# Diagonal blocks stored turned, the first two units substituted in buffers of their own, and a new hand-written order, in a delta-rule attention followed by a token and channel mixer

## The chip, the cores and the metric

The kernel runs on one core of a Trainium2 chip, in float32. The core has a matrix engine (PE; its weight loads are listed as PEld), a vector engine (DVE), a scalar engine (ACT), a general engine (POOL) and a queue that issues transfers (SP). Each engine runs its own instructions in the order in which the program lists them and waits for the others by semaphores. The metric is the device time of one execution in microseconds (us).

## The reference

First an attention block: per batch and head a state of 48x48 is updated token by token, each key normalized. Then a mixer: a low-rank product over tokens and a two-layer network over channels.

```python
B, H, S, D = 4, 8, 768, 48
k_n = k / (np.linalg.norm(k, axis=-1, keepdims=True) + 1e-06)
for t in range(S):
    y[:, :, t] = q[:, :, t] @ state                       # per batch and head
    v_old = state.T @ k_n[:, :, t]
    state = state + beta[t] * outer(k_n[t], v[t] - v_old)
x = y.transpose(0, 2, 1, 3).reshape(B, S, H * D)          # (4, 768, 384)
u = x + ((x.transpose(0, 2, 1) @ U) @ V).transpose(0, 2, 1)   # U (768, 32), V (32, 768)
out = u + np.maximum(u @ w_ch1, 0.0) @ w_ch2              # 384 -> 1536 -> 384
```

## The kernel before

**Chunks and units.** Tokens are cut into 12 chunks of 64 per batch. A *unit* is six chunks of one batch with all eight heads; there are eight units, n = 0 to 7, two per batch, and units take turns in two large buffers, `slots` (slot 0 for even n, slot 1 for odd n). Within a chunk the token-by-token update is written as a triangular system of 64x64 (keys times keys, scaled by beta), whose inverse is needed; then the chunk's effect on the state is a few matmuls.

**Preparing a unit.** Loads of k, q, v (`load`, `name` "z" is a second copy of odd heads of k) go to the slot. For units 0 to 2, PE turns k and q (`turn`, L672) and ACT and DVE copy the result (`placed`, L682 to L687); later units are turned by DVE (`turn_blocks`, L747). `products` (L700) multiplies keys with keys (i = 0) and keys with queries (i = 1), for two halves j of the heads. For i = 0 the two 32x32 diagonal blocks of each 64x64 product are brought into a tile `diag` (L710 on ACT for the upper block, L713 twice on DVE for the lower one, with a mask `even`); ACT then copies the whole product (L720) and, for units 0 and 1, splits it by rows (L724). For i = 1 DVE masks the product (L731), once per parity of the heads.

`blocks` inverts the diagonal blocks. A DVE transposition (L794) spreads them so that each partition holds one block in `gs`; `norms` takes the norms from their diagonals (ACT's square root L619, five small DVE steps L622 to L627, the turned norms L633, the scaling of v L636); L798 scales; then `substituted` runs size - 1 steps, each a DVE product (L803) and a DVE subtraction (L809), on `gs` and `xt`. For units 0, 1 (`SPLIT`) and 2 (`QUARTERED`) the blocks are halved first, 15 steps on 16x16; the others do 31 steps on 32x32. POOL clears `xt` beforehand (`seed`, L788). L816 transposes the inverse back into `zz`, and L825 makes its turned copy. All units use the same `gs`, `xt`, and one buffer for the products of the steps.

`joins` puts the inverses together to 64x64: for the halved units with two rounds of small matmuls (L860, L874) with ACT copies (L835, L865) and a DVE step (L878) between; for all with four phases of 32x32 matmuls (L900/L903, L918/L921), ACT copies between them (L908, L927, L939) and POOL clears (L946). `prepare` applies the inverse to k and v (L1023, L1034 on PE; L1042, L1047 on ACT).

**The recurrence** (`recur`) walks through the 12 chunks of a batch: L1072 (PE) and L1085 (DVE) make z from the state s, L1100 (PE) and L1111 (DVE; L1113 for the first) the next state, L983 and L997 the outputs, which ACT puts into X (L967). The chunks 0 to 5 need unit 2b, the chunks 6 to 11 unit 2b + 1.

**Weights.** U, V and the two layers' weights come in as pairs of words (L1186; 14 pieces, i = 0 for U, 1 for V, then 6 and 6) and are converted by one ACT scaling (L1198) and three DVE passes (L1212, L1219, L1226). A landing buffer serves several pieces in turn, so a later load waits for an earlier piece's last pass. The second layer is then combined by eight DVE differences (L1141).

**The mixer** of a batch starts when its 12 chunks are in X: `front` (L1393, L1399, L1412, L1417, L1436, L1439), then the channels (L1497, relu L1462) and the second layer (L1617, L1537) for three blocks of 256 tokens. While batch b is mixed, batch b + 1 goes through preparation and recurrence on the same PE. For the last batch, L1296 and L1617 run alone at the end.

**The order.** Every routine yields its next step, and a table `ORDER` says which routine's step is emitted at each place; 2259 places. `run` only follows the table (the costs in `op(...)` don't decide anything any more). Since each engine works in emission order, the table is what sets each engine's queue.

## Time and profile before

| | us |
|---|---|
| time, median of three runs | 599.11 |
| the three runs | 602.46, 598.93, 599.11 |
| span of the profiled execution | 594.9 |
| PE busy, share | 559.7, 94% |
| DVE busy, share | 409.3, 69% |
| ACT busy, share | 216.8, 36% |
| POOL busy, share | 133.3, 22% |
| first matmul of the mixer's channels (L1497) starts at | 115.95 |
| granted PE clock 0.50 | 31.8 to 86.4 and 93.3 to 103.5 |

The span is one profiled execution, from its first to its last instruction; the runs' times are of executions of the whole program, and their median is 4.2 us above this span. Times in the text count from the span's start. Busy time of PE is a union over overlapping matmuls whose ends are modelled. The granted clock is the share of full speed that PE had. In rows of the groups, the figures behind the bar are busy us, mean ns of one instruction, and the idle time of the engine just before.

### The profile page before, as it was taken

Reading aid. Unit: us, or ns where it says so; the run is one execution under the profiler, and the core shown is the slowest. Engines: PE = TensorE matmul, PEld = TensorE weight load, DVE = VectorE, ACT = ScalarE, POOL = GpSimd, SP = SyncE. Lnnn points to the kernel's source line nnn. Section 1 sums busy time; section 2 is a strip of 40 time slices with the busy share of each in tenths; the row PEclk is TensorE's granted clock in tenths of the full one; section 3 lists DMA queues with packets and bytes.
Section 4 is the critical chain, followed back from the end, with each engine's and each line's share of the span. In section 5 each row is a group of like instructions: output and inputs, shape, how many; then the busy total and the mean of one; then the engine's idle time right before and its main releaser. Section 6 shows DMA issues by size and latency. Waiting matters only on the chain.

```text
span 594.9 us, 23426 instructions
## 1 busy us (share of the span) xinstructions
PE 559.7 (94%) x10428; PEld 481.6 (81%) x10428; DVE 409.3 (69%) x1011; ACT 216.8 (36%) x442; POOL 133.3 (22%) x229
## 2 busy tenths in 40 slices
PE   3778978899999999999999999999999999999997
PEld 3578977678988887989889887889899868656997
DVE  3888758899999458999884279998883235313542
ACT  1846475446322542035224341252243321335000
POOL 8122036116010724141205214520310000000000
PEclk9855556999999999999999999999999999999999
DMA  9981639714030415240402144420401000000000
GB/s 140 180 176 24 214 80 197 152 56 79 3 65 12 68 31 92 46 91 13 82 2 43 18 83 90 79 56 2 95 7 43 4 2 4 16 8 1 26 28 28
DMA packets 89445, 36.23 MB, mean 61 GB/s; under 512 B 75456, under 2 KB 87104, under 8 KB 89344
## 3 DMA queue, kind: packets, MB, share of 16 engines
q1 hardware_dynamic: 80800, 24.69, 20.7%
q0 software_dynamic: 6944, 9.74, 8.3%
q8 instruction: 82, 1.34, 1.0%
q10 hardware_dynamic: 1600, 0.30, 0.3%
q14 instruction: 19, 0.16, 0.1%
HBM read 29.98 MB, written 4.72 MB: 58 GB/s over the span
## 4 chain that ended last, share of the span: by engine, by line
PE 83%; DVE 11%; issue 2%; ACT 2%; DMA 1%; SPq 0%; DVEq 0%; ACTq 0%
PE P L1617 27%; PE P L1497 22%; PE P L1296 7%; PE P L700 4%; DVE xt L809 3%; DVE prod L803 3%; PE P L1072 2%; PE P L860 2%; PE P L874 2%; PE P L1023 2%; PE P L1034 2%; PE P L983 2%; PE P L997 2%; PE P L1100 2%; PE P L1412 2%
## 5 line engine op out<-in xcount | busy, mean ns | idle before, releaser
L1497 PE MATMUL P<-ut,w_sb 128*128 128x256 f32 x648 | 150.1, 385 | 1.5 <-ACT ut L1439 0.9
L1497 PEld LDWEIGHTS P<-ut,w_sb 128*128 128x128 f32 x648 | 119.9, 190 | 18.7 <-ACT ut L1439 1.1
L1617 PE MATMUL P<-w_sb,hs 128*128 128x192 f32 x540 | 96.7, 331 | 0.1
L1617 PEld LDWEIGHTS P<-w_sb,hs 128*128 128x128 f32 x540 | 87.2, 190 | 3.7 <-issue 1.2
L809 DVE TENSOR_TENSOR xt<-xt,prod 128x112 f32<-128x112 f32 (+21 forms) x200 | 64.6, 323 | 6.9
L803 DVE TENSOR_TENSOR prod<-gs,xt 128x112 f32<-128x112 f32 (+21 forms) x200 | 63.3, 316 | 3.5
L1537 DVE TENSOR_TENSOR X<-X,P 128x192 f32<-128x192 f32 x84 | 29.1, 349 | 49.8 <-PE P L1617 49.4
L1462 ACT ACTIVATE hs<-P 128x512 f32<-128x512 f32 x54 | 32.2, 598 | 77.5 <-PE P L1497 65.6
L967 ACT COPY X<-P 64x192 f32<-64x192 f32 x96 | 30.0, 313 | 66.3 <-PE P L997 63.4
L1617 PE MATMUL P<-w_sb,S 128*128 128x192 f32 x288 | 50.7, 330 | 0.0
L1617 PEld LDWEIGHTS P<-w_sb,S 128*128 128x128 f32 x288 | 46.6, 190 | 2.8 <-issue 1.8
L555 POOL DMA_DIRECT2D slot<-in_v_dram x32 | 21.1, 664 | 92.3 <-DVE prod L803 60.3
L1085 DVE TENSOR_TENSOR z<-slot,P 128x192 f32<-128x192 f32 x44 | 15.5, 352 | 30.8 <-PE P L1072 29.7
L541 POOL DMA_DIRECT2D slot<-in_q_dram x40 | 24.6, 621 | 46.9 <-DVE slot L747 33.3
L939 ACT COPY slot<-zz 32x384 f32<-32x384 f32 x64 | 32.4, 509 | 7.0 <-DVE zz L878 3.9
L700 PE MATMUL P<-slot 48*64 48x64 f32 x1536 | 30.9, 231 | 2.1 <-issue 1.4
L1296 PE MATMUL P<-slot,w_sb 128*128 128x384 f32 x96 | 32.9, 486 | 0.0
L700 PEld LDWEIGHTS P<-slot 48*64 48x64 f32 x1536 | 27.9, 144 | 5.6 <-issue 2.7
L946 POOL MEMSET slot<- 32x384 f32 x32 | 13.3, 421 | 84.2 <-PE P L903 63.4
L1617 PE MATMUL P<-w_sb,slot 128*128 128x192 f32 x180 | 30.4, 327 | 0.9 <-DVE X L1537 0.9
L555 POOL DMA_DIRECT2D slot<-in_k_dram x44 | 29.4, 670 | 8.3 <-PE P L1100 7.6
L1617 PEld LDWEIGHTS P<-w_sb,slot 128*128 128x128 f32 x180 | 29.3, 190 | 1.7 <-DVE X L1537 1.5
(153 smaller groups left out, 901.4 us busy)
## 6 DMA issues: line engine op xcount, KB each, us to landing
out_dram<-X SPq DMA_DIRECT2D x22, 192.0 KB, 2.7
w_sb<-in_moe_w_ch_dram SPq DMA_DIRECT2D x10, 384.0 KB, 5.6
slot<-in_k_dram SPq DMA_DIRECT2D x48, 72.0 KB, 3.9
slot<-in_k_dram POOLq DMA_DIRECT2D x44, 72.0 KB, 3.8
slot<-in_v_dram SPq DMA_DIRECT2D x32, 72.0 KB, 3.7
slot<-in_v_dram POOLq DMA_DIRECT2D x32, 72.0 KB, 3.5
X<-in_moe_w_ch_dram SPq DMA_DIRECT2D x6, 384.0 KB, 6.1
wide<-in_moe_w_ch_dram SPq DMA_DIRECT2D x6, 384.0 KB, 5.0
```

Source lines behind the costliest of these rows:

```text
L541: queue.dma_start(out=blocked(n)[quarter(y % 4), j, g, :, 0:w], in_=src[b, 4 * g + 2 * j + par, hf * UC * L : (hf + 1) * UC * L, BK * low ...
L555: queue.dma_start(out=t[half(1 - g if name == "z" else g), :, to, 0:D], in_=src[b, 4 * g + s, hf * UC * L : (hf + 1) * UC * L, :].rearrang ...
L700: nc.tensor.matmul(p_g[half(g ^ (par * i)), par, c], kq[rows, c, j, 0, half(g)], kq[rows, c, j, i, half(g)], start=True, stop=True,)
L803: nc.vector.tensor_tensor(out=prod, in0=gb[:, :, j : j + 1, j + 1 :].to_broadcast([128, split, m, w]), in1=xb[:, :, 0:m, j : j + 1].to_bro ...
L809: nc.vector.tensor_tensor(out=xb[:, :, 0:m, j + 1 :], in0=xb[:, :, 0:m, j + 1 :], in1=prod, op=ALU.subtract,)
L939: nc.scalar.copy(pg[quarter(i), :, at, :, a : a + BK], cut(zc, h)[quarter(i)].rearrange("p r (c j) t -> p r c j t", j=2),)
L967: nc.scalar.copy(x[half(c % 2), c // 2, 4 * D * g : 4 * D * (g + 1)].rearrange("p (j r d) -> p r j d", r=2, d=D), states(p_y)[half(g)],)
L1296: nc.tensor.matmul(to, w, t, start=start, stop=stop, skip_group_check=True)
L1462: nc.scalar.activation(hs[:, fs[0] : fs[1] + 1 : fs[1] - fs[0]], p_f, ACTF.Relu)
L1497: nc.tensor.matmul(p_f[:, x], w(x, t), ut[:, t], start=(t == 0), stop=(t == KT - 1))
L1537: nc.vector.tensor_tensor(out=to, in0=to, in1=p, op=ALU.add)
L1617: nc.tensor.matmul(to, of[0], of[1], start=of[2], stop=of[3], skip_group_check=True)
```

## The change

1. The tile `diag` holds its blocks with the element index outermost instead of innermost, so that the DVE transposition out of it reads consecutive elements. It is filled by four copies of 32 partitions each (for units 0 and 2 to 7 two on ACT and two on DVE, for unit 1 all on ACT) instead of one masked ACT pass and two masked DVE passes.
2. The transposition back reads `xt` in its own order and writes the turned copy in `zz` first; the other copy is made from it by the smaller transposition. For the halved units the ACT copies `part` start from the returned inverse directly.
3. The mask of q products is one DVE pass over both parities.
4. Unit 1 has its own two buffers (in a part of the second layer's weight tile that is not in use yet) and its own product buffer; the units' waits follow from that (`ahead`). Unit 2 waits for unit 0 there, later units for the one before.
5. For units 0 and 1 the product and the subtraction of a step are separate places of the table, so that other DVE instructions can stand between them.
6. `ORDER` is new as a whole, 2289 places. Unit 0's k is loaded first (SP's and ACT's first four issues), then unit 1's; POOL clears both units' buffers at the start, ahead of its loads; the load of U and its ACT scaling and first two DVE passes stand ahead of the diagonal copies. Unit 0's q products stand behind its joining on PE. All weights are converted and combined on DVE before the last chunk of batch 0's recurrence (before: after it too). The two preparations of unit 1 stand in one piece.

```diff
-        diag = slot[:, 6144 : 6144 + BK * BK].rearrange("p (q t) -> p q t", t=BK)
+        diag = slot[:, 6144 : 6144 + BK * BK].rearrange("p (t q) -> p q t", t=BK)
...
+    room = w2_sb.rearrange("p m f d -> p (m f d)")[:, 0 : 2 * (BK + 1) * BK].rearrange(
+        "p (z s t) -> p z s t", z=2, t=BK
+    )
+
+    def grams_of(n):
+        return room[:, 0] if n == 1 else gs
+
+    def inverse_of(n):
+        return room[:, 1] if n == 1 else xt
+
+    def ahead(n):
+        return n - 1 if n > 2 else -1 if n < 2 else 0
...
-                yield op("act", act(384) + 0.1, rush=True)
-                nc.scalar.mul(to, p_g[:, :, :, 0:BK], even[:, 0:1])
-                for r in range(2):
-                    yield op("dve", dve(192) + 0.05, rush=True)
-                    nc.vector.scalar_tensor_tensor(
-                        out=to[:, r], in0=p_g[:, r, :, BK:L], scalar=even[:, 1:2], in1=to[:, r],
-                        op0=ALU.mult, op1=ALU.add,
-                    )
+                for y in range(4):
+                    rows, cols = quarter(y), quarter(y % 2)
+                    if n == 1 or y % 2 == 0:
+                        yield op("act", act(384) + 0.05, rush=True)
+                        nc.scalar.copy(to[rows], p_g[rows, :, :, cols])
+                    else:
+                        yield op("dve", dve(384), rush=True)
+                        nc.vector.tensor_copy(out=to[rows], in_=p_g[rows, :, :, cols])
...
-                for par in range(2):
-                    yield op("dve", dve(384), give=[("pair", x)] if par else ())
-                    nc.vector.tensor_tensor(
-                        out=qk[:, par, :, j],
-                        in0=p_g[:, par],
-                        in1=mask_u[:, None, :].to_broadcast([128, UC, L]),
-                        op=ALU.mult,
-                    )
+                yield op("dve", dve(768), give=[("pair", x)])
+                nc.vector.tensor_tensor(
+                    out=qk[:, :, :, j],
+                    in0=p_g,
+                    in1=mask_u[:, None, None, :].to_broadcast([128, 2, UC, L]),
+                    op=ALU.mult,
+                )
...
-            yield need(("returned", n - 1))
+            yield need(("returned", ahead(n)))
             yield op("pool", 1.05)
-            nc.gpsimd.memset(xt, 0.0)
+            nc.gpsimd.memset(x_n, 0.0)
...
-        yield need(*[("diag", n, j) for j in range(2)], ("substituted", n - 1))
-        yield op("dve", 2.0)
-        nc.vector.transpose(gs[:, 0:BK], diag.rearrange("p q t -> p t q"))
+        yield need(*[("diag", n, j) for j in range(2)], ("substituted", ahead(n)))
+        yield op("dve", 1.25)
+        nc.vector.transpose(g_n[:, 0:BK], diag.rearrange("p q t -> p t q"))
...
+            if lone:
+                yield op("dve", dve(split * m * w), port=True)
             nc.vector.tensor_tensor(
                 out=xb[:, :, 0:m, j + 1 :], in0=xb[:, :, 0:m, j + 1 :], in1=prod,
...
         nc.vector.transpose(
-            zz[:, 0 : BK * BK].rearrange("p (q t) -> p t q", t=BK),
-            xt[:, 0:BK].rearrange("p s t -> p t s"),
+            zz[:, CS * BK : CS * BK + BK * BK].rearrange("p (q s) -> p s q", s=BK),
+            x_n[:, 0:BK],
         )
...
-        def turned(h):
-            nc.vector.transpose(cut(zn, h), cut(zc, h))
+        def turned(h, back=False):
+            to, of = (zc, zn) if back else (zn, zc)
+            nc.vector.transpose(cut(to, h), cut(of, h))
...
         def part(h):
 
             to = parted(h).rearrange("p (r e) t -> p r e t", r=2)
+            yield need(("returned", n))
...
-            yield op("dve", dve(384), lat=-dve(384) if split == 2 else None)
-            turned(h)
+            yield op("dve", dve(384))
+            turned(h, True)
             if split == 2:
-                if lone:
-                    begin(part(h), place_of(n))
-                else:
+                if not lone:
                     emitted(("parted", n, h))
...
         for h in range(2):
             begin(diagonals(h), place_of(n))
+            if lone:
+                begin(part(h), place_of(n))
             begin(joins(h), place_of(n))
```

The rest of the diff is the table `ORDER`, which is replaced whole, and the same substitutions in `norms`.

433 lines of the change are left out of this document (222 added, 211 removed).

## The prediction

> **What bounds the kernel now.** I read four views: the page's slices, the busy time by stretch, the chain of waits, the timelines of DVE, ACT and PE. The slices show three ages: PE (the matrix engine) has holes and half its clock up to about 103 us, then it is full to the tail.
>
> ```profile
> PE   3778978899999999999999999999999999999997
> ...
> DVE  3888758899999458999884279998883235313542
> ...
> PEclk9855556999999999999999999999999999999999
> ```
>
> Busy time by stretch (columns PE, weight loads, DVE, ACT, POOL, then the granted clock) says the same in numbers:
>
> ```profile
> 30.00:35.00 5.00, 1.66 (x57) 1.55 (x58) 4.86 (x14) 0.68 (x1) 0.83 (x1) 0.68 1.18 239
> ...
> 65.00:70.00 5.00, 5.00 (x155) 4.81 (x148) 5.00 (x11) 2.58 (x7) 0.00 (x0) 0.50 0.93 306
> ...
> 116.00:560.00 444.00, 440.40 (x7636) 371.83 (x7637) 312.26 (x770) 152.96 (x317) 92.53 (x155) 1.00 0.21 41
> ```
>
> From 116 us PE idles 3.6 us in 444: nothing that makes DVE, ACT or POOL cheaper there is worth more than that. What can move is the instant when the mixer starts. The chain of waits has it in one line, and the DVE timeline has the stations before it:
>
> ```profile
> 115.95 8.04 PE P L1497 x36
> ```
>
> ```profile
> 18.66 1.97 DVE L794 STREAM_TRANSPOSE gs<-slot 128x1024 f32<-128x1024 f32 x1
> ...
> 32.09 1.95 DVE L816 STREAM_TRANSPOSE zz<-xt 128x1024 f32<-128x1024 f32 x1
> ...
> 61.93 0.36 DVE L1113 COPY s<-P 128x192 f32<-128x192 f32 x1 [0.84 <-PE P L1100]
> ...
> 88.94 0.35 DVE L1085 TENSOR_TENSOR z<-slot,P 128x192 f32<-128x192 f32 x1 [1.34 <-PE P L1072]
> ...
> 106.96 0.35 DVE L1085 TENSOR_TENSOR z<-slot,P 128x192 f32<-128x192 f32 x1 [0.61 <-PE P L1072]
> ```
>
> So, before: unit 0's diagonal blocks complete at 18.55 (last L713), its inverse returned at 34.04, first state at 61.93, chunk 6 (unit 1's first) at 88.94, chunk 11 at 106.96, mixer at 115.95; the end is 478.9 later, at 594.9. PE issues nearly the same matmuls before the first mixer matmul in both programs (1342 and 1346), so the end moves with the mixer's start.
>
> **The change, part by part.** Durations, from the groups by line:
>
> ```profile
> L747 DVE STREAM_TRANSPOSE slot<-slot 128x384 f32<-128x384 f32 x40 | 21.8, 562 | 1.3 <-DMA slot<-in_k_dram 1.0
> L816 DVE STREAM_TRANSPOSE zz<-xt 128x1024 f32<-128x1024 f32 x8 | 16.6, 2075 | 0.3
> L731 DVE TENSOR_TENSOR slot<-P,mask_u 128x384 f32<-128x384 f32 x32 | 17.4, 544 | 0.1
> L794 DVE STREAM_TRANSPOSE gs<-slot 128x1024 f32<-128x1024 f32 x8 | 15.7, 1962 | 0.2
> L713 DVE SCALAR_TENSOR_TENSOR slot<-P,even,slot 128x192 f32<-128x192 f32 x32 | 12.3, 408 | 3.6 <-ACT slot L710 3.5
> ```
>
> *Transpositions.* The 128x128 one takes 0.286, the 128x384 one 0.562: 1.08 ns an element, so 1024 elements read in a row cost 0.562 + 640 x 1.08 ns = 1.25. L794, which reads in steps, takes 1.96; it becomes 1.25. L816 reads and writes in steps, 2.08; after, it only writes so. Low end 1.25, high end 1.96 (a stepped write as dear as a stepped read); I take 1.35, since the stepped write adds only 0.11 to L794's row. DVE saves about 8 x (0.71 + 0.73) = 11.5.
>
> The Trainium skill (SBUF — State Buffer, Door 1) says that SBUF has 16-byte lines and that each access crossing to a new line pays; it names no exemption for writes. L794 against L747 agrees for reads. By that rule L816's successor keeps 1.96 and the copies into the diagonal tile, which now write in steps of 32 elements, pay too.
>
> *Diagonal copies.* One ACT pass (0.58) and two DVE passes (0.41 each) per unit and pair become four 32-partition copies, two on ACT and two on DVE, for unit 1 all on ACT. Nearest rows: ACT's 32x384 copy 0.51 (L939), DVE's 128x384 copy from PSUM 0.56 (L684); high end 0.27 more each (384 x 0.7 ns, the stepped read's price). I take 0.51 and 0.56. DVE: +0.30 x 14 pairs - 0.82 x 2 = +2.6; ACT: +0.44 x 14 + 1.46 x 2 = +9.1, beside other work after 116 us. *Masking q*: one pass over 768 elements (0.946 by L1417's like row) for two of 0.544: -0.14 x 16 = -2.3.
>
> *Own buffers, single steps.* On DVE unit 1's transposition still stands behind unit 0's return, so the buffers alone start nothing earlier. The split lets conversions stand between a product and its subtraction. Dependent steps start 0.03 after the end of the one before (0.29 long, 0.32 apart); an unrelated one starts 0.08 before it (29.77 + 0.26, next at 29.95). About 0.1 for each place filled, some 2 in all.
>
> Station by station, in the new order of each queue:
>
> *Diagonal blocks.* k of unit 0 goes out as SP's first four issues (0.74 each, done at 3.8) and ACT's four (done at 3.6). The load that released PE's first matmul took 4.96; the second head pair then lands near 8.8 (before, its transposition ran at 14.55). Transposition, copy and product (0.9, 0.5, 0.9 by these rows) end near 11.5. But ACT's scaling of the mixer's U (L1198) and two of its DVE passes now stand in front of the diagonal copies. U's load is POOL's third issue, behind one beta and one q load and two 1.0 us clears (L788), done at 7.0 instead of 15.4. Before, it took 9.7 behind fifteen loads; the median of all slot loads is 3.9. I take 5.0: U at 12.0, then 0.4 and four ACT copies, DVE 0.5 and four of its own: complete at **15.0** (-3.5). Ends: 13.5 and 19.2.
>
> *Return of unit 0.* 1.25 + 2.26 (norms and scaling, as before) + 8.65 (30 steps; 22.89 to 31.86 before, with three conversions in it) + 0.3 + 1.35: **28.8** (-5.2).
>
> *First state.* PE begins joining behind one more half turn, at 29.4 (34.19 before). Its cold rows: L860 5.3, L874 5.3, q products 1.5, then the four 32x32 phases with ACT between them, to 46. DVE waits meanwhile for the first L874, to 37.3. Two q products of unit 0, which before filled PE's idle time ahead of 34, now come here (3.0 cold), and ACT has two head splits (L724, 0.6) and a scaling (0.9) in front of the last L927s: preparing starts at 50.3 and 51.2 (50.5 and 55.35 before), PE is ready at 57.8. DVE's queue from 43.6 on holds the rest of unit 1's steps, the vn scaling, three masks, four and a half weight conversions (0.55 + 0.94 + 1.02) and the return: 15.1 with each 0.08 shorter: **58.7** (-3.2). So 2.0 of the 5.2 is given back.
>
> *To chunk 6.* Weight conversions and the second layer's differences (L1141, 0.74 each), which before ran until 140 us, stand between the recurrence's steps. Adding the queue gap by gap, none under the 1.3 that a step through PE took: 24.7 to chunk 5's z (21.5 before), 4.9 more to its state. PE now prepares both halves of unit 1 in one piece, 6.0 at half clock (L1023 1.5, L1034 1.45, twice): chunk 6 at 90.8, or 89.3 if the clock rises at 86.4 as it does now. I take **90.0** (+1.1).
>
> *To the mixer.* Five steps: 2.6, 2.6 and, with six transpositions of unit 2 each (0.9 at full clock), two of 3.0, one of 4.8: 16.0 (18.0 before), chunk 11 at **106.0** (-1.0). The front is as long as before (9.0): mixer at 115.0. Later, four more changes of matmul shape (151 for 147) cost 0.1 to 0.2 each (12 L1497 take 2.79, 72 take 15.74), and the earlier second-layer weights may close 1.0 of the 3.6 idle: -0.5. Sum -1.5 on 594.9: 593.4, and 4.2 around the span (median 599.1 less 594.9) give **597.5**. The three runs span 3.5, so I call 1% (6 us) what can be told from no change.
>
> **Rivals.**
>
> *The clock rises early (faster).* 31.8 to 86.4 is at 0.50 though PE is busy 5.00 of 5.00. Denser joining could lift it. Then DVE's queue is the floor: 43.9 instead of 47.3 from first state to chunk 11, and up to 4.5 more before it. Half of that second part: 592; all: 589.5. Against: 55 to 70 was as dense and stayed at half. The Trainium skill (TensorE: Matmul & The Clock Gate, Part 1) says some 3.4 us of sustained activity releases the full clock; the rows at 65 to 70 contradict it, so I keep its chance at 0.20.
>
> *Conversions hold the recurrence (slower).* Every weight scaling waits for a buffer freed a few conversions earlier, 384 KB pieces (5.0 to 7.8 to land, 1.3 to issue, 0.9 on ACT). Before chunk 5's state the last such load has about 6.5. It costs once the turnaround exceeds that: three waits of 2 to 3 us give 604. For it: 86.73, where a conversion waiting for ACT already held DVE 2.96. Chance 0.17.
>
> *U lands late, or stepped writes are dear* (the layout then only moves the strides): 19.2 for the diagonals, or +1.1 for copies and +0.6 for the return. Either loses 2 to 4: 601. Chance 0.12.
>
> *The earlier start survives whole* (PE and ACT hide the conversions): -3.2 to -5: 593. Chance 0.08. My forecast has 0.43.
>
> **Chances.** Range 588.5 to 606, the first two rivals' ends. Under 593.1: most of the first rival, half of the fourth, the lower edge of the forecast, 0.28. Over 605.1: half of the second, part of the third and losses of a wholly new order that I can't name, 0.20. Between: 0.52.
>
> **What shows it.** The two large transpositions at 1.25 and 1.35; diagonal copies ending near 15; return near 29; first state near 59; both preparations in one piece near 85 to 90; the mixer at 115. A mixer start off by over 5 us with PE still full behind it would mean that a station was mis-summed; holes in PE after it would make the whole frame wrong.

## The result, and the profile after

The changed kernel takes 616.75 us (median of four runs, 613.54 to 619.82), the kernel before 599.02 beside it. The ratio is 1.0304, with a 95% interval from 1.0244 to 1.0364: slower. The forecast was 597.5, with a range up to 606.

The slices of the profile after (PE, DVE, granted clock):

```profile
PE   4876978779999998998999999998999999999997
...
DVE  5989895776996438899896269999973134323532
...
PEclk9956556789999999899999999999999999999999
```

PE has lost its unbroken row of nines behind the start, and the clock dips once more in it. Busy time by stretch (PE, weight loads, DVE, ACT, POOL, granted clock):

```profile
30.00:35.00 5.00, 3.81 (x102) 3.49 (x99) 3.36 (x7) 4.89 (x10) 4.36 (x7) 0.83 1.13 195
65.00:70.00 5.00, 5.00 (x128) 4.96 (x130) 3.65 (x8) 3.05 (x6) 0.00 (x0) 0.50 0.56 170
116.00:560.00 444.00, 429.80 (x7668) 360.65 (x7667) 298.70 (x732) 156.51 (x312) 94.72 (x159) 0.99 0.20 40
```

In the last stretch PE is now idle for 14.2 us where it was for 3.6 (1.3 of the 14.2 lie ahead of the mixer's start, which has moved to 124.84). The groups after that answer to the rows of before (busy us, mean ns, idle time ahead of them and what ended it):

```profile
L739 DVE COPY slot<-P 32x384 f32<-32x384 f32 x28 | 22.5, 819 | 10.9 <-ACT slot L736 10.4
...
L753 DVE TENSOR_TENSOR slot<-P,mask_u 128x768 f32<-128x768 f32 x16 | 15.0, 943 | 1.4 <-PE P L723 1.4
L841 DVE STREAM_TRANSPOSE zz<-xt 128x1024 f32<-128x1024 f32 x7 | 13.8, 1970 | 0.1
...
L736 ACT COPY slot<-P 32x384 f32<-32x384 f32 x36 | 28.8, 820 | 28.8 <-PE P L723 21.0 <-DVE slot L739 7.5
L743 ACT COPY slot<-P 128x768 f32<-128x768 f32 x16 | 12.6, 797 | 4.5 <-DVE slot L739 4.5
```

The copies into the turned tile take 0.82 on both engines, and the two engines wait for each other: DVE's copies stood idle 10.4 us for ACT's, ACT's 7.5 us for DVE's, and ACT's copy of the whole product (L743) 4.5 us more. The stations on DVE:

```profile
15.68 1.25 DVE L817 STREAM_TRANSPOSE gs<-slot 128x1024 f32<-128x1024 f32 x1
...
28.01 1.96 DVE L841 STREAM_TRANSPOSE zz<-xt 128x1024 f32<-128x1024 f32 x1
...
61.06 0.36 DVE L1140 COPY s<-P 128x192 f32<-128x192 f32 x1
...
94.39 0.34 DVE L1112 TENSOR_TENSOR z<-slot,P 128x192 f32<-128x192 f32 x1
...
107.53 0.79 DVE L739 COPY slot<-P 32x384 f32<-32x384 f32 x1 [3.14 <-ACT slot L736]
108.36 0.35 DVE L1112 TENSOR_TENSOR z<-slot,P 128x192 f32<-128x192 f32 x1
108.74 2.49 DVE L739 COPY slot<-P 32x384 f32<-32x384 f32 x3
111.26 0.35 DVE L1138 TENSOR_TENSOR s<-s,P 128x192 f32<-128x192 f32 x1
...
113.83 0.36 DVE L1112 TENSOR_TENSOR z<-slot,P 128x192 f32<-128x192 f32 x1 [1.06 <-PE P L1099]
```

| us | before | forecast | after |
|---|---|---|---|
| unit 0's diagonal blocks complete | 18.55 | 15.0 | 15.57 |
| unit 0 returned | 34.04 | 28.8 | 29.97 |
| first state | 61.93 | 58.7 | 61.06 |
| chunk 6 (z) | 88.94 | 90.0 | 94.39 |
| chunk 11 (z) | 106.96 | 106.0 | 113.83 |
| first mixer matmul | 115.95 | 115.0 | 124.84 |
| from there to the end | 478.9 | 478.4 | 493.3 |
| span | 594.9 | 593.4 | 618.1 |

So the 23.2 us of span lie in two places: 8.9 ahead of the mixer's start, where the forecast had -0.9, and 14.4 behind it, where it had -0.5. Some of this is the choice of executions: the profiled one of the changed kernel was the longest of its four (spans from 611.9 to 618.1), and by the medians the loss is 17.7. Behind the mixer's start, what PE waited for up to 560 (us in total, times, longest; "issue" is a gap in which the profile names no wait), first before, the three largest rows:

```profile
PE P L1497 <- ACT ut L1439: 0.9, 1, 0.9
PE P L983 <- DVE s L1111: 0.6, 1, 0.6
PE P L1497 <- issue: 0.6, 1, 0.6
```

and in the changed kernel, the five largest:

```profile
PE P L1524 <- ACT hs L1489: 2.6, 2, 2.0
PE P L899 <- issue: 2.1, 1, 2.1
PE P L925 <- ACT slot L743: 1.6, 2, 1.2
PE P L1050 <- ACT X L994: 0.9, 1, 0.9
PE P L1127 <- ACT slot L743: 0.7, 1, 0.7
```

All of these five but "issue" are waits for ACT. In the whole view 7.4 us are waits for ACT, 2.5 for DVE and 2.1 "issue".

### The profile page after: what moved, and what is told of

Its sections match the earlier page's. It is cut to its first block, busy times and chain, and to the rows that moved or that the text cites. A ratio compares the mean times of both kernels' runs of the same rounds, so it can differ in the third digit from the quotient of the medians.

```text
span 618.1 us, 23455 instructions
## 1 busy us (share of the span) xinstructions
PE 572.2 (93%) x10428; PEld 489.3 (79%) x10428; DVE 414.2 (67%) x991; ACT 236.5 (38%) x462; POOL 133.9 (22%) x229
## 4 chain that ended last, share of the span: by engine, by line
PE 68%; DVE 18%; ACT 5%; DMA 5%; issue 3%; SPq 1%; DVEq 0%; ACTq 0%
PE P L1644 25%; PE P L1524 16%; PE P L1323 7%; PE P L723 3%; DVE xt L834 2%; DVE prod L826 2%; PE P L1099 2%; DMA slot<-in_k_dram 2%; DVE slot L739 2%; DVE zz L841 2%; DMA wide<-in_moe_V_dram 2%; PE P L899 2%; PE P L1010 2%; PE P L1061 2%; PE P L1420 2%
## 5 line engine op out<-in xcount | busy, mean ns | idle before, releaser
L1524 PE MATMUL P<-ut,w_sb 128*128 128x256 f32 x648 | 154.0, 389 | 2.6 <-ACT hs L1489 2.6
L1644 PEld LDWEIGHTS P<-w_sb,hs 128*128 128x128 f32 x540 | 88.9, 193 | 3.5 <-DVE X L1564 1.2
L834 DVE TENSOR_TENSOR xt<-xt,prod 128x31 f32<-128x31 f32 (+20 forms) x185 | 60.8, 328 | 6.3
L826 DVE TENSOR_TENSOR prod<-gs,xt 128x31 f32<-128x31 f32 (+20 forms) x185 | 59.9, 324 | 3.4
L1489 ACT ACTIVATE hs<-P 128x512 f32<-128x512 f32 x54 | 32.0, 598 | 48.2 <-PE P L1524 41.5
L564 POOL DMA_DIRECT2D slot<-in_k_dram x40 | 24.4, 619 | 78.5 <-ACT X L994 29.2
L736 ACT COPY slot<-P 32x384 f32<-32x384 f32 x36 | 28.8, 820 | 28.8 <-PE P L723 21.0
L964 ACT COPY slot<-zz 32x384 f32<-32x384 f32 x64 | 32.3, 508 | 18.1 <-DVE zz L851 11.0
L723 PE MATMUL P<-slot 48*64 48x64 f32 x1536 | 33.6, 244 | 4.8 <-issue 1.7
L723 PEld LDWEIGHTS P<-slot 48*64 48x64 f32 x1536 | 30.0, 156 | 9.9 <-issue 4.7
```

What stands on the lines that cost most here:

```text
L564: queue.dma_start(out=blocked(n)[quarter(y % 4), j, g, :, 0:w], in_=src[b, 4 * g + 2 * j + par, hf * UC * L : (hf + 1) * UC * L, BK * low ...
L723: nc.tensor.matmul(p_g[half(g ^ (par * i)), par, c], kq[rows, c, j, 0, half(g)], kq[rows, c, j, i, half(g)], start=True, stop=True,)
L736: nc.scalar.copy(to[rows], p_g[rows, :, :, cols])
L826: nc.vector.tensor_tensor(out=prod, in0=gb[:, :, j : j + 1, j + 1 :].to_broadcast([128, split, m, w]), in1=xb[:, :, 0:m, j : j + 1].to_bro ...
L834: nc.vector.tensor_tensor(out=xb[:, :, 0:m, j + 1 :], in0=xb[:, :, 0:m, j + 1 :], in1=prod, op=ALU.subtract,)
L964: nc.scalar.copy(pg[quarter(i), :, at, :, a : a + BK], cut(zc, h)[quarter(i)].rearrange("p r (c j) t -> p r c j t", j=2),)
```

## The experiments

Two theories stood at the start. **A**: the four copies into the turned tile cost the time, because other work that PE waits for stands behind them on ACT and DVE. **B**: the new table does, whatever a copy takes. Others came as these were met (C to F below). All kernels, with the mixer's start and what lies behind it from one profiled execution each (PE idle: its gaps of over 0.02 between matmul records; half clock: half the length of the windows with a granted clock of 0.50):

| kernel | median | ratio to before, 95% | mixer starts | to the end | PE idle | half clock |
|---|---|---|---|---|---|---|
| before | 599.02 | | 115.95 | 478.9 | 4.4 | 0 |
| after | 616.75 | 1.0304 [1.0244, 1.0364] | 124.84 | 493.3 | 13.8 | 3.4 |
| e1 straight diag | 609.24 | 1.0167 [1.0134, 1.0201] | 119.85 | 487.1 | 10.2 | 1.7 |
| e2 masked diag | 603.53 | 1.0072 [1.0031, 1.0113] | 118.54 | 483.0 | 7.0 | 1.7 |
| e3 turned diag alone | 615.46 | 1.0273 [1.0224, 1.0323] | 121.48 | 489.3 | 11.8 | 0.3 |
| e4 turned, units 0, 1 | 605.55 | 1.0102 [1.0070, 1.0134] | 120.70 | 483.3 | 7.2 | 2.0 |
| e5 join filled | 601.25 | 1.0058 [1.0032, 1.0085] | 119.32 | 480.6 | 5.8 | 0 |
| e6 split preparation | 603.99 | 1.0111 [1.0062, 1.0160] | 117.38 | 482.8 | 6.7 | 1.7 |
| e7 both moves | 601.42 | 1.0057 [1.0025, 1.0089] | 119.94 | 479.6 | 5.4 | 0.4 |
| e8 copies on DVE | 634.36 | 1.0566 [1.0494, 1.0637] | 127.76 | 506.9 | 21.0 | 12.2 |
| e9 copies on ACT | 622.41 | 1.0391 [1.0331, 1.0450] | 127.29 | 492.6 | 13.8 | 3.6 |
| e10 first k alone | 598.65 | 0.9994 [0.9961, 1.0028] | 113.22 | 480.9 | 4.7 | 2.2 |
| e11 whole copy first | 613.83 | 1.0245 [1.0191, 1.0298] | 125.17 | 486.5 | 8.7 | 3.4 |
| e12 the same, masked | 608.03 | 1.0142 [1.0099, 1.0186] | 121.89 | 484.2 | 8.8 | 0 |
| e13 straight, on ACT | 603.47 | 1.0092 [1.0061, 1.0122] | 119.72 | 479.9 | 4.3 | 0 |
| e14 behind chunk 11 | 606.86 | 1.0151 [1.0104, 1.0199] | 121.23 | 485.1 | 4.3 | 5.3 |
| e15 with its bank | 601.76 | 1.0066 [1.0039, 1.0093] | 119.08 | 485.0 | 5.6 | 4.6 |
| e16 front ahead too | 605.82 | 1.0125 [1.0077, 1.0174] | 116.92 | 483.5 | 5.5 | 3.5 |
| e17 first k and norms | 596.32 | 0.9983 [0.9952, 1.0015] | 112.28 | 483.7 | 6.2 | 3.4 |

The sum of a row is its profiled span, which is not its median: single executions of the kernel before lay between 593.60 and 603.05. So how large a difference is, is read from the medians and their intervals; where it arises, from the traces.

### Part 1 taken apart: e1, e2, e3, e4

e1 undoes one line of the changed kernel:

```diff
-        diag = slot[:, 6144 : 6144 + BK * BK].rearrange("p (t q) -> p q t", t=BK)
+        diag = slot[:, 6144 : 6144 + BK * BK].rearrange("p (q t) -> p q t", t=BK)
```

> The changed kernel with one line undone: the tile diag has its element index innermost again, so the four copies write consecutive elements and the large transposition reads in steps. Same table, same instructions. Theory A (the stepped writes of the copies cost the time, since ACT and DVE work in order and PE waits for what stands behind them): the copies fall from 0.82 (ACT) and 0.75 (DVE) to about 0.52 and 0.56, the transposition L817 rises from 1.25 to 1.96; after the mixer's start PE's gaps fall from 12 to under 6 and the run gains 8 to 14 us: 603 to 609. Theory B (the new table costs the time, whatever a copy takes): the copies get shorter just so, the run moves by under 3 us: 614 to 618.

e2 undoes the whole part in the changed kernel's table (unit 1 keeps its four copies, straight):

```diff
-                        nc.scalar.copy(to[rows], p_g[rows, :, :, cols])      # y = 0, 2
-                        nc.vector.tensor_copy(out=to[rows], in_=p_g[rows, :, :, cols])   # y = 1, 3
+                        nc.scalar.mul(to, p_g[:, :, :, 0:BK], even[:, 0:1])  # y = 0
+                        nc.vector.scalar_tensor_tensor(...)                   # y = 1, 3: r = 0, 1
```

> The changed kernel with part 1 undone as a whole for all units but unit 1: straight layout, one masked ACT pass (0.58) and two masked DVE passes (0.41 each) at three of the four places of the table; unit 1 keeps four copies on ACT, into the straight layout. Theory A: ACT loses 14 x (1.64 - 0.58) = 15 us and DVE 14 x (1.5 - 0.82) = 9.5 us of queue time against the changed kernel, PE's gaps after the mixer's start go back to 4 or 5 us: 598 to 606. Theory B: the table's order keeps the mixer at 121 or later and the gaps behind it: 611 to 618.

e3 is the other way round, the kernel before with this part alone:

```diff
-        diag = ... "p (q t) -> p q t"
+        diag = ... "p (t q) -> p q t"
-                nc.scalar.mul(to, p_g[:, :, :, 0:BK], even[:, 0:1])
+                for y in (0, 2):
+                    nc.scalar.copy(to[quarter(y)], p_g[quarter(y), :, :, quarter(0)])
-                    nc.vector.scalar_tensor_tensor(...)
+                    nc.vector.tensor_copy(out=to[quarter(y)], in_=p_g[quarter(y), :, :, quarter(1)])
```

> The kernel before, with part 1 alone: the turned layout and the four copies, two on ACT at the place of the masked ACT pass, one on DVE at the place of each masked DVE pass; the large transposition then reads consecutive elements (1.25 for 1.96), the return is as before. Theory A: 16 x 1.06 = 17 us more on ACT, 16 x 0.68 - 8 x 0.71 = 5 us more on DVE, PE finds its operands late as in the changed kernel: 606 to 614. Theory B: the copies lie beside other work in the order before, the shorter transpositions make up for them: 597 to 602.

e4 is e2 with the changed kernel's layout and copies for units 0 and 1:

```diff
+        if n > 1:
+            diag = ... "p (q t) -> p q t"      # and the masked passes of e2
```

> The changed kernel with the turned layout and the four copies for units 0 and 1 only (the two for which the recurrence of batch 0 waits at the start); units 2 to 7 have the straight layout and the three masked passes. If the copies of units 2 to 7 cost the time behind the mixer's start (14.4 us), this is 603 or below and no slower than with all units masked; if the copies matter ahead of the mixer, it is slower than that one by 1 to 4 us; by theory B it is 611 to 618.

Part 1 alone, in the old table, costs 2.73%; the changed kernel without it 0.72%, and that is the new table together with parts 2 to 5, which were not taken apart. Theory A holds, in both tables, though e1 (609.24) and e3 (615.46) lie just outside its ranges; what is left for B is about a quarter of the loss. The sizes come from the groups. e1, straight copies:

```profile
L736 ACT COPY slot<-P 32x384 f32<-32x384 f32 x36 | 16.7, 468 | 27.2 <-PE P L723 21.6 <-DVE slot L739 5.2
...
L739 DVE COPY slot<-P 32x384 f32<-32x384 f32 x28 | 15.3, 556 | 7.7 <-ACT slot L736 7.2
...
L817 DVE STREAM_TRANSPOSE gs<-slot 128x1024 f32<-128x1024 f32 x7 | 13.7, 1960 | 0.4
```

e3, turned ones:

```profile
L711 ACT COPY slot<-P 32x384 f32<-32x384 f32 x32 | 26.2, 819 | 15.4 <-PE P L700 15.0
...
L718 ACT COPY slot<-P 128x768 f32<-128x768 f32 x16 | 12.8, 799 | 12.6 <-DVE slot L714 12.5
...
L714 DVE COPY slot<-P 32x384 f32<-32x384 f32 x32 | 26.2, 819 | 10.8 <-ACT slot L711 10.3
...
L792 DVE STREAM_TRANSPOSE gs<-slot 128x1024 f32<-128x1024 f32 x8 | 9.9, 1234 | 0.2
```

Writing in steps raises a copy out of the matrix engine's memory from 0.468 to 0.819 on ACT and from 0.556 to 0.819 on DVE. A pair of products saves 0.72 at the transposition and pays 4 x 0.35 on ACT and 4 x 0.26 on DVE for it: the layout moves the strides from one read to eight writes. That is e1 against the changed kernel, 7.5 us by the medians. The other 5.7 (e1 to e2) are four copies of 0.5 for a pass of 0.58 and two of 0.41.

e4 places them: the turned copies of units 0 and 1 cost 2.2 ahead of the mixer and nothing behind it (120.70 for 118.54, 483.3 for 483.0); those of units 2 to 7 cost 4.1 ahead (2.1 of it by chunk 11, among whose steps unit 2's copies stand) and 10.0 behind. These are profiled executions; by the medians units 0 and 1 cost 2.0, units 2 to 7 11.2.

### Which queue: e8, e11, e9

ACT is 20 us busier than before (236.5 for 216.8) and still idle for 62% of the span, DVE 5 us (414.2 for 409.3). Why does this cost PE anything? One case from the timelines of DVE, ACT and PE in the changed kernel:

```profile
277.26 1.96 DVE L841 STREAM_TRANSPOSE zz<-xt 128x1024 f32<-128x1024 f32 x1
279.25 1.04 DVE L851 STREAM_TRANSPOSE zz<-zz 128x384 f32<-128x384 f32 x2
...
279.92 0.51 ACT L964 COPY slot<-zz 32x384 f32<-32x384 f32 x1 [4.25 <-DVE zz L851]
280.33 0.58 ACT L1489 ACTIVATE hs<-P 128x512 f32<-128x512 f32 x1
...
280.97 1.56 PE L1524 MATMUL P<-ut,w_sb 128*128 128x256 f32 x6 [2.00 <-ACT hs L1489]
```

DVE's return and its turned copy end late, since three copies (L739, at 271.8 to 275.7) stand among the last steps of the substitution ahead of them. ACT's next instruction, a copy of what is returned (L964), waits 4.25 for them, the relu behind it (L1489) waits with it, and PE waits 2.00 for the relu. ACT and PE have time to spare there, DVE has none: from 260 to 280 it is busy for 19.05 of 20.00 us, ACT for 5.98. Each works in the order written, so what lengthens DVE's queue holds up the other two.

Which of the two queues counts was tried by moving the copies of units 2 to 7, turned as in the changed kernel: all four to DVE (e8), all four to ACT (e9), or behind the whole copy, reading from it (e11).

```diff
-                    if n == 1 or y % 2 == 0:
+                    if n == 1 or n == 0 and y % 2 == 0:     # e8; the else branch is DVE's copy
```

> The changed kernel with all four turned copies of units 2 to 7 on DVE; ACT has none of them any more (12 products, 20 us less on ACT, 20 us more on DVE). The trace of the changed kernel shows the four copies of a product one after the other, ACT, DVE, ACT, DVE, then L743, each waiting for the one before: DVE idled 10.4 us for L736 in 9 cases, ACT 7.5 us for L739 in 9 and 4.5 more ahead of L743. Theory C (the length of this chain counts, 4 x 0.8 + 0.9 from product to L743, since PE waits for L743 or for the bank that it frees): the chain is as long as before, the run stays at 612 to 618. Rival (ACT's queue counts: its two copies stand in front of relu and X): PE's waits for ACT go, 604 to 609.

```diff
                     if n == 1 or y % 2 == 0:
+                        if n > 1 and y == 0:                # e11
+                            nc.scalar.copy(pg[:, :, :, j], p_g)
-                        nc.scalar.copy(to[rows], p_g[rows, :, :, cols])
+                        nc.scalar.copy(to[rows], pg[rows, :, :, j, cols])   # n > 1; DVE's likewise
```

> The changed kernel with the order within a product turned round for units 2 to 7: ACT first copies the whole product (L743), ahead of the four turned copies, and these read it from there instead of from the bank. Same engines, same number of copies, same turned layout. Theory C: L743 comes 0.9 after the product, the bank is free then, nothing of PE waits for the four copies any more; most of the loss behind the mixer's start (10 of 14.4 us) goes: 603 to 608. Rival (the time of the copies on the queues counts, wherever they stand): 613 to 618.

```diff
-                    if n == 1 or y % 2 == 0:
+                    if n > 0 or y % 2 == 0:                 # e9
```

> The changed kernel with all four turned copies of units 2 to 7 on ACT (as unit 1 has them): ACT 20 us more, DVE 19 us less, no ACT copy of a product waits for DVE any more. With all four on DVE the run took 634 us, and PE's waits for ACT rose from 7 to 13 us although ACT had less to do: what PE waited for was ACT's L743 and the relu behind it, and ACT waited for DVE. Theory D (ACT waiting in order for DVE's copies is what costs, since DVE's queue is the full one): with ACT alone the chain is 4 x 0.82 + 0.8 = 4.1, no longer than in the changed kernel, but nothing of DVE's queue is in it, and DVE's chunks 10 and 11 have no copies in front: 606 to 613. Rival E (ACT's time counts as much as DVE's): 20 us more on ACT cost as much as 20 us more on DVE did: 628 to 636.

e8 and e9 came out as neither of their theories had it; e11 (613.83) lies at the lower edge of its rival's range. e8 was dearest by far, 634.36. Its groups:

```profile
L964 ACT COPY slot<-zz 32x384 f32<-32x384 f32 x64 | 32.3, 508 | 24.7 <-DVE zz L851 16.6 <-DVE zz L903 7.0
...
L743 ACT COPY slot<-P 128x768 f32<-128x768 f32 x16 | 12.5, 796 | 22.7 <-DVE slot L739 22.7
```

Its largest wait of PE behind the mixer's start:

```profile
PE P L1524 <- ACT hs L1489: 7.4, 4, 4.7
```

ACT has less to do and stands 22.7 us in front of L743 for DVE's copies (4.5 in the changed kernel). So it is not ACT's own time that counts, as e8's rival had it; and the chain from product to L743 is not just four copies long, as theory C had it, since the copies stand in DVE's queue behind everything else there.

e11 takes L743 out of that chain, and by the trace C is right about what it can see: PE's waits for L743 are gone, those for relu fall from 2.6 to 1.1, and from the mixer's start to the end it takes 486.5 instead of 493.3. Ahead of the mixer nothing is gained (125.17), and the median falls by 2.9 only, with intervals that overlap. e11 also changes a second thing: 24 of DVE's copies now read the core's own memory and take 0.517 for 0.819, some 7 us less in DVE's queue. So C is at most one part and not "most", and how much of the gain in the profiled execution is the order, and how much the shorter copies, is not shown.

e9, with DVE out of all of it, is 5.7 slower than the changed kernel by the medians, at the edge of what can be told (the two intervals just overlap). Behind the mixer's start it is level (492.6); the loss is ahead, at chunk 10. ACT's timeline there, then PE's:

```profile
105.86 4.04 ACT L736 COPY slot<-P 32x384 f32<-32x384 f32 x5 [0.56 <-PE P L723]
109.91 0.31 ACT L994 COPY X<-P 64x192 f32<-64x192 f32 x1
...
111.24 0.57 PE L1127 MATMUL P<-z,slot 64*48 64x48 f32 x16 [4.53 <-ACT X L994]
```

The state's matmuls wait 4.53 for a bank, which two short copies into X have to empty, and these stand behind five and one more of the turned copies. In the changed kernel DVE's z stands behind one of its copies at the same place, and the next state behind three more (107.53 to 111.26 above). So theory D (only ACT's waiting for DVE costs) and rival E (time costs alike on both) both fall. What is left is **F**, made after these runs and so not tested by them: a copy costs what is queued behind it on its engine, at each place by itself; on DVE that is most, since the returns, z and s, and through them ACT's queue, stand there.

Straight copies, all on ACT, in the old table were the test of D there (units 1 to 7, on top of e10, below):

```diff
+                for y in range(4) if n else ():
+                    nc.scalar.copy(to[quarter(y)], p_g[quarter(y), :, :, quarter(y % 2)])
                 for r in range(2):
                     yield op("dve", dve(192) + 0.05, rush=True)
+                    if n:
+                        continue
                     nc.vector.scalar_tensor_tensor(
```

> The kernel before with unit 0's k first (598.7 us), and for units 1 to 7 the diagonal blocks brought over by four straight copies, all on ACT at the place of its masked pass (4 x 0.46 for 0.58), none on DVE (13 x 0.82 = 11 us less there); layout, transpositions and table as before, unit 0 masked as before. Theory D: ACT's chain to the whole copy is 1.85 + 0.8 and waits for no DVE queue, before it was 0.58 + 0.82 on DVE + 0.8: level behind the mixer's start, and DVE's chunks 10 and 11 lose 1.5 us of passes in front of them: 595.5 to 598. Rival E: ACT's 17 us more cost like DVE's: 603 to 610.

It is D's forecast behind the mixer's start (479.9, PE idle for 4.3) and E's for the sum: with the copies of units 1 and 2 in ACT's queue, unit 0 returns at 34.33 instead of 32.67, and chunk 10 to 11 takes 8.8 instead of 6.0. So four copies of 0.46 cost nothing in one part of the run and a few us in another.

### What the table costs by itself: e5, e6, e7, e12

e2 is still 0.72% slower than before. Its trace has PE's largest gap and two more just ahead of it in one place, the first joining of unit 2 (124.6 to 128.8), with a half-clock window behind them:

```profile
PE P L906 <- issue: 1.7, 1, 1.7
...
PE P L892 <- DVE zz L858: 0.6, 1, 0.6
...
PE P L906 <- ACT zz L897: 0.5, 1, 0.5
```

e5 moves two places of the mixer's channels in among these small matmuls:

```diff
-channels b0 i0 e2: 637 646;
+channels b0 i0 e2: 620 624;
-joins n2 h0: 614 620 621 622 623 625 626 627 638 ...
+joins n2 h0: 614 621 622 623 625 627 628 629 639 ...
```

> The kernel with straight, masked diagonals in the new table (603.5 us, span 601.5), with two places of the table moved: the two halves of the mixer's third pair of channel blocks (L1531, six matmuls each) now stand among the first two rounds of unit 2's joining (L892 and L906), one ahead of the first round, one between its two halves and the second. Theory B1 (what the table still costs behind the mixer's start is this one place: PE idles 0.63 for the returned block, 0.47 for ACT's copy and 1.70 with nothing to wait for in the profile, while the joining's small matmuls run alone, and a window of 3.4 us at half clock follows): the three gaps shrink from 2.8 to under 1.0, the window goes, the run gains 2.5 to 4: 599.5 to 601. Rival (the gaps only move to the next small matmuls): 602.5 to 604.

e6 splits the two preparations of unit 1 and moves conversions and differences behind chunk 6:

```diff
-prepare n1 h0: 442 459 460 461;
-prepare n1 h1: 443 462 463 480;
+prepare n1 h0: 442 443 444 445;
+prepare n1 h1: 459 464 465 476;
-load_weights: ... 426 438 457 458;
+load_weights: ... 426 438 463 470;
-sums f0: 427 447 448 474;  sums f3: 469 486 490 494
+sums f0: 427 480 483 487;  sums f3: 497 504 505 515
```

> The kernel with straight, masked diagonals in the new table, with the places between chunk 5's state and chunk 10 rearranged: chunk 6 waits only for the preparation of the first half of unit 1's chunks, the second half's preparation stands in PE's queue after chunk 6's z and state; on DVE the last weight conversions and the eight differences of the second layer stand behind chunk 6's z and state and in the idle time of the later steps. Theory B2 (the table holds the recurrence there): z of chunk 6 moves from 92.4 to about 89, of chunk 11 from 109.5 to 107, the mixer's start from 118.5 to 116, the run gains 2 to 3: 600.5 to 601.5. Rival (PE's work ahead of the mixer is the same and the steps wait for it later): the mixer starts at 118 or later, 603 to 604.

e7 has both.

> Both rearrangements at once. If the two places are all that the new table costs beside the diagonal copies, this is 597 to 599, level with the kernel before; if the returns of the two units, 2 and 5 us earlier than before, come through, 595 to 597; by the two rivals 602 to 604.

e5: the gaps fall from 2.8 to 1.5, the half-clock window is gone, the stretch behind the mixer's start is 2.4 shorter; the median by 2.3, just short of what was expected, and by the ratios to before (1.0072 and 1.0058) the two can't be told apart. e6: chunk 6 comes at 89.2 as its theory said, but the lead of 3.2 has shrunk to 1.2 by chunk 11 (108.4), and the median does not move (603.99). That is its rival's time, though the mixer starts at 117.38, between the two forecasts; the rival's reason, that PE's work ahead of the mixer is the same and the steps wait for it later, was not tested by itself. e7 does no better than e5 and lies between its forecasts. So what is left without part 1, some 0.6%, was only in part found.

e12 puts the whole copy ahead of the masked passes in e7, as e11 did in the changed kernel:

> The kernel with both moves of the table and straight, masked diagonals (601.4 us), with the whole copy ahead of the three masked passes for units 2 to 7, which read it. Theory C says that the chain there is 2.3 long and becomes 0.9: what waits of PE are left for it (under 1.5 us behind the mixer's start) go, 599.5 to 601. If the runs of ACT and DVE were only shifted: 601 to 602.

It lost 6.6 by the medians (some 5 by the ratios to before) where a gain or nothing was expected: DVE's passes now stand idle 13.4 us for ACT in all, 6.0 in e7, and z and s stand behind them (chunk 11 at 110.8 for 108.5, of which 1.6 was there at chunk 9, ahead of them; PE's gaps behind the mixer's start 8.8 for 5.4, the largest new one for X).

### Unit 0's k first, alone, and what the order gives back: e10, e14 to e17

```diff
-load n0 namek halves(0,): 2 7 15 16        # SP; table of the kernel before
+load n0 namek halves(0,): 1 2 3 4
-turn n0 i0 j0 namek: 17;  turn n0 i0 j1 namek: 34;  turn n1 i0 j0 namek: 22
+turn n0 i0 j0 namek: 20;  turn n0 i0 j1 namek: 21;  turn n1 i0 j0 namek: 34
```

> The kernel before with the third named part alone: unit 0's k goes out first on SP (its four issues, then z, then unit 1's k), and PE turns and multiplies all of unit 0's k ahead of unit 1's first half; all other places of the table as before. Unit 0's diagonal blocks then end about 2 to 2.5 earlier (18.55 to about 16). If this lead reaches the mixer, the run gains 1 to 2.5: 595.5 to 597. If it is used up by unit 1, whose k lands later, or by DVE's queue ahead of the first state: 597.5 to 599.

Of the two parts tried alone (e3 and e10) this is the one that costs nothing. Unit 0's blocks are complete at 13.6, though the transposition still begins at 16.5 (18.66 before), behind unit 1's passes on DVE; the first state comes at 59.4, the mixer starts at 113.2, 2.7 earlier. The median is 0.8 below the 599.43 of before beside it, with 1 inside the interval: nothing that can be told from no change.

F was then tried by places alone. e14 moves chunks 10 and 11 ahead of unit 2's transpositions, products and passes in e10; e14 also gives one step another bank of the matrix engine's memory, and e15 is e14 with other banks for three steps; e16 moves the mixer's front ahead as well and has none of these other banks. No instruction is added. The core of the edits:

```diff
 recur b0: ... 429                            # state of chunk 9
+recur b0: chunk 10's z and s, chunk 11's z;  outputs b0 c8 to c11     # e14
+front b0 i0 (between unit 2's steps)                                 # e16
 turn, placed, products n2 i0 j0, j1;  load_weights (three passes)
-recur b0: chunk 10's z and s, chunk 11's z
```

> The kernel before with unit 0's k first (598.7 us, mixer's start 113.2), with the places between chunk 9's state and chunk 11 rearranged: the z and state of chunk 10, the z of chunk 11 and their outputs stand ahead of unit 2's transpositions, products and diagonal passes on PE, ACT and DVE, and ahead of four of the weight conversions' passes on DVE. No instruction is added or left out. Theory F (copies and conversions cost what stands behind them in the same in-order queue, whichever engine it is, and this is the place ahead of the mixer where they stand in front of the recurrence): chunk 10 to 11 takes about 3 instead of 6.0, chunk 11's z comes at 100 instead of 104.2, the mixer's start moves to about 109.5; behind it unit 2 is 3 to 4 later, which PE's mixer work covers: 595 to 597. Rival (unit 2's later blocks open holes behind the mixer's start, or PE's work ahead of the mixer is the bound): 597.5 to 600.

> The kernel with unit 2's products behind chunk 11 (606.9 us), with other banks of the matrix engine's memory for three later places: the mixer's reserved bank is no longer the one that unit 2's last masked q product holds. In the run before, chunk 11's z came at 101.66 as its theory expected (104.23 without the move), but the first mixer matmul, at 121.2, had waited 4.55 for DVE's mask of that product, since both used one bank. Theory F: without that wait the mixer starts at 112 to 113.5, behind it nothing changes: 596 to 599. Rival (unit 2's later blocks are what holds the mixer, by whatever bank): 602 or more.

> The kernel before with unit 0's k first, chunks 10 and 11 ahead of unit 2's products, and now the mixer's front for the first block too (L1811, tt, L1830, X, L1854, ut in the places between unit 2's transpositions, products and passes instead of behind them). In the run before this one chunk 11's z came at 101.4 as expected, and the front began only 6.8 later, behind unit 2's transpositions and products on PE, and waited 1.9 for its tt on DVE behind unit 2's passes and transposition: what is queued behind the copies paid, now the front in place of the chunks. Theory F: the first mixer matmul comes at 109 to 111 (113.2 with the first k alone): 594 to 598. Rival (PE needs its time for the same work, and half the clock until it has been busy for long: the start stays at 113 or later): 598 to 602.

Chunk 11 came at 101.7, 101.4 and 101.0 (104.2 in e10): the place does cost what F says, 2.6 to 3.2 us there. But the mixer came at 121.2, 119.1 and 116.9, later than in e10, each time for something that now stood behind the moved copies: in e14 a bank held by unit 2's last product (4.55), in e15 the front, as PE's timeline has it,

```profile
108.19 2.14 PE L1813 MATMUL P<-X,u_sb 128*32 128x384 f32 x24 [0.67 <-ACT slot L1140]
...
113.01 0.88 PE L1832 MATMUL P<-tt,v_sb 64*64 64x384 f32 x8 [1.88 <-DVE prod L1223]
```

and in e16 unit 2's q products, which waited 2.40 for an ACT copy ahead of the first mixer matmul. The forecasts of 594 to 599 for these failed, and e14 and e16 came out above their rivals' ranges too. The traces show one reason: each forecast looked at the next wait only.

e17 tries a lead at the very start instead, in e10: unit 0's own steps ahead of unit 1's.

```diff
-DVE: unit 1's two masked passes, unit 0's transposition, betas, norms
+DVE: unit 0's transposition, betas, norms, unit 1's two masked passes
-ACT: whole copy of unit 1, beta_rows, whole copy of unit 0, root of the norms
+ACT: whole copy of unit 0, beta_rows, root of the norms, whole copy of unit 1
```

> The kernel before with unit 0's k first, and unit 0's own steps ahead of unit 1's first half: on DVE unit 1's two masked passes stand behind unit 0's transposition and norms (in the run with the first k alone this transposition began at 16.5, behind them, though unit 0's blocks were complete at 13.6; the norms waited until 18.7 for beta's copies, which stood on ACT behind unit 1's whole copy), on ACT unit 0's whole copy, beta's copies and the norms' root stand ahead of unit 1's whole copy. No instruction is added. Theory F at the start of the path: transposition at 13.7, norms done by 18 instead of 20, unit 0 returns at 30 instead of 32.7, the mixer starts at 110.5 to 112 (113.2 with the first k alone): 595.5 to 597.5. Rival (DVE's queue ahead of the first state, or the preparation of unit 1, takes the lead back): mixer at 113 or later, 598 to 600.

The transposition begins at 13.5, the first state comes at 57.8 and the mixer starts at 112.3, 3.7 earlier than before and at the edge of what was expected. In the profiled execution the stretch behind is 4.8 longer than before: PE's "issue" gaps there are 3.4 in all, for 1.1, and one of 1.41 at 230.5 is followed by 6.8 us at half clock. The median, 596.32, is the lowest of the study and inside its forecast, but only 0.7 below the 597.01 of before beside it, and again not told from it (0.9952 to 1.0015); so the hit says little for F. So no kernel here was measurably faster than the one before.

## Why the prediction was wrong

**The station sums of the start held to within 2.4.** Diagonal blocks (15.57 for 15.0), return (29.97 for 28.8), first state (61.06 for 58.7; 59.13 with masked passes). U landed in time. L817 takes 1.25 as said; the single pass over q 0.943 for 0.946; the straight copies 0.468 and 0.556 for 0.51 and 0.56.

**Mis-sized: the stepped write.** For the copies 0.51 and 0.56 were taken and 0.27 more kept as the upper end. Measured are 0.82 and 0.82, above that end on ACT (0.78) and just below it on DVE (0.83). The return was put at 1.35, it takes 1.97, its upper end; this is the whole miss of unit 0's return beyond that of its blocks. The Trainium skill (SBUF — State Buffer, Door 1) has each access that crosses to a new 16-byte line pay. The rows agree for writes: ACT's copy 0.819 for 0.468, the return 1.97 for 1.25. A return that both reads and writes in steps took 2.08, hardly more: the two do not add up, so the 0.11 by which it exceeded L794's row was no measure of a stepped write. One row limits this: in e11 DVE's stepped copy took only 0.517 when it read the core's own memory. The terms that the prediction gives for DVE add up to 11.2 us less work; its busy time rose by 4.9. The copies (28 x 0.26) and the returns (8 x 0.62) are 12.3 of this difference of 16.1.

**The step that failed: "beside other work after 116 us", priced at nothing.** The prediction had the copies' 9.1 us on ACT there (ACT's busy time rose by 19.7), and the third rival ("stepped writes are dear") priced them at 1.1, counting unit 0 only: 601. By e4 the copies of units 2 to 7 alone cost 14.1 us of span, 11.2 by the medians. The only reason that it gives is that PE idles 3.6 in 444, so that nothing there can be worth more. This bounds what a cheaper instruction can bring. It says nothing of what a dearer one costs: a full PE is full because the others' results come in time, with little to spare in queues that may not be overtaken. The mean over the stretch hid this too: before, DVE was busy for 69% of the span, but for 18.74 of 20.00 us from 245 to 265. e8 and e13 give both ends: 20 us moved from ACT to DVE cost 17.6, as much moved from DVE to ACT (e9) 5.7, and straight copies on ACT (e13) nothing behind the mixer's start.

**Chunk 6 and the steps to chunk 11.** Forecast 90.0 and 16.0, measured 94.39 and 19.4; with masked passes 92.37 and 17.2. The copies of unit 2 were not in this sum, though they stand between chunks 10 and 11 in the DVE queue that it walked through; what remains at chunk 6, 2.4, goes when the preparation in one piece and the conversions are moved (e6, 89.2).

**The rivals.** The clock rose no earlier: 33.3 to 57.1 and 60.6 to 91.3 were at 0.50. Conversions held the recurrence less than thought: e6 took them out of the way, and the lead was gone by chunk 11. The sentence that holes behind the mixer's start would make the whole frame wrong was the right one to write down; it gave such holes no chance of their own. The range's ends, 588.5 and 606, are called the first two rivals' ends, but those are given as 589.5 and 604.

What stays open: some 0.6% that is left without part 1, in the new table or in parts 2 to 5, and what PE does in its long "issue" gaps (1.3 to 2.1 us each in the joining and elsewhere).

## What to carry to other kernels

An engine that idles under 1% bounds the gain from the others' work, not the loss: before adding even cheap work to a half-idle engine, look at what stands behind it in that queue and who waits for that, and how busy it is in that stretch and not on average. Choosing a layout for one reader, count the writers: here one read of 1024 elements saved 0.72 us and eight copies paid 2.4 for it. Moving work within a tuned order pays at the next wait, so price a move up to the end of the path and not to the station behind it.

## What was not expected of the hardware

- A lost microsecond of PE can cost a second one. Behind the mixer's start PE is busy 97% of the changed kernel's time, and yet windows at half clock appear after clusters of holes: 3.2 us of gaps between 130.9 and 135.5 are followed by one of 3.4 us at 135.7, in e8 five times (some 12 us lost, half of the windows' length, beside 21.0 of gaps). When e5 had cut the first cluster from 2.8 to 1.5, none came. The gaps alone do not decide it, though: the same four of 0.08, 0.08, 0.65 and 0.24 were followed by such a window in the changed kernel (from 242.6, window at 248.3) and in e10 (from 225.5, window at 231.4), and by none in the kernel before (from 228.1). The Trainium skill (TensorE: Matmul & The Clock Gate, Part 1) puts the return to half clock at an idle window of about 3.4 us; in the changed kernel no single gap behind the start was longer than 2.1.
- In e11, where the stepped copies read the core's own memory instead of the matrix engine's, DVE took 0.517 for one, against 0.798 (0.819 in the changed kernel), ACT 0.856 against 0.816:

```profile
L741 ACT COPY slot<-slot 32x384 f32<-32x384 f32 x24 | 20.6, 856 | 0.6
L741 ACT COPY slot<-P 32x384 f32<-32x384 f32 x12 | 9.5, 816 | 1.0 <-PE P L723 0.7 <-DVE slot L746 0.2
...
L746 DVE COPY slot<-slot 32x384 f32<-32x384 f32 x24 | 12.1, 517 | 11.1 <-ACT slot L739 10.8
L746 DVE COPY slot<-P 32x384 f32<-32x384 f32 x4 | 2.9, 798 | 0.3 <-ACT slot L741 0.2
```
- In the changed kernel the copies of one product by two engines ran one after the other, although they read and wrote different partitions: the waiting ones wait for a semaphore of the one before. This order is the program's; what the engines would do without these semaphores was not tried.
